# A transformer block with adaLN: the first turn's weights taken in separate steps by score slots, and two output copies moved to GpSimd

## The chip, the cores and the metric

One core of one Trainium2 chip runs the whole kernel. The metric is the device time of one execution in microseconds (us). Engines are named as in the profile: PE is TensorE, DVE VectorE, ACT ScalarE, POOL GpSimd, SP SyncE. SyncE computes nothing here: it issues every DMA, in the order of its queue, and an issue whose condition isn't met holds all behind it. All engines take their instructions in the order of their queues.

## What is computed

```python
mod = (silu(c) @ w_mod).reshape(1, 6, 1, 576)        # sa, ca, ga, sb, cb, gb
h = layernorm(x) * (1 + ca) + sa                     # x: 2048 x 576, float32
q, k, v = h @ wqkv                                   # 32 heads of 18
p = softmax(q @ k.T * 18 ** -0.5)
x = x + ga * ((p @ v) @ wo)
h = layernorm(x) * (1 + cb) + sb
x = x + gb * (silu(h @ w1) @ w2)                     # w1: 576 x 4608, w2: 4608 x 576
```

Matmuls keep float32's accuracy by three products of two-part numbers: a weight `w` is split into a high part in fp32r and the rest, and so is the activation; high x high, high x rest and rest x high are summed.

## The kernel before

The 2048 queries go in four blocks of 512. For each block all 32 heads are taken in eight quads of four heads. A **score slot** is one step of attention: a matmul of scores for the maxima of a later part (`psa`, reduced on VectorE, L728), and one of scores with the maximum already subtracted (`psb`, L776), whose exponential ScalarE takes into `pt` (L778); matmuls with the values (`psv`, L813) follow. A quad of a block has 64 slots, a block 512. What follows attention (projection with `wo`, layernorm, the MLP) for block b is dealt out as filler between the slots of block b+1. I call the slots of block 1, 2 and 3, with the MLP of the block before in them, the first, second and third **turn**; the MLP of block 3 runs alone at the end.

The MLP has 36 first-layer weights (128 hidden units each, tile `w1t`) and 36 second-layer ones (`w2t`). The filler takes **pairs** of first-layer weights (`mlp1`, L1011 and after), with their results through SiLU in tiles `g`, and after two pairs the second layer of a **chunk** of four (`mlp2`). Pairs are counted from 0: pair 0 opens the MLP, pair 2 stands just ahead of the first second-layer group, and pairs 3 and 17 bound the later chunks of the turn. The results of the second layer are added to `x`: one half by VectorE (L918); the other is copied by ScalarE into one of two buffers `gt` (L921) and added by GpSimd (L922). Of a pair's two results, ScalarE and VectorE form SiLU in buffers `etmp`, ScalarE writes the high part of `g` (L1037), and GpSimd subtracts it for the rest (L1038), which frees an `etmp` buffer. ScalarE's queue holds all this between the exponentials.

In the first turn the weights come as float32. `weights` (L633) loads each in two halves into a ring of three buffers `raw`, on GpSimd multiplies a half of a second-layer weight by `gb` (L646), casts it to the high part (L647) and subtracts that for the rest (L648), and at its next call stores the split weight to device memory. From the second turn on one DMA loads the stored weight. The order of TensorE's instructions is that of the program, which a planner (`Plan`, the loop at L1476 and after) makes from estimated costs; the other engines' queues are put in order by a scheduler, which moves a load, split or store up to where it thinks that its inputs and buffers are ready.

At the start of a turn the last quad's output is moved by DMAs from `ov` into the rows of `ou` (L841), `o_T` copies each of five blocks `kt`, four of 128 rows and one of 64, into `th` on ScalarE (L894) and forms the rests `tl` on GpSimd (L897), that of the fifth on VectorE (L899), and the projection `psp` follows.

## Time and profile before

| | us |
|---|---|
| median of three runs | 2437.68 (2436.85 to 2441.84) |
| the profiled execution | 2447.21 |
| its span | 2445.4 |
| TensorE busy in the span | 2352.7 (96%) |
| VectorE / ScalarE / GpSimd busy | 1783.8 / 1483.1 / 631.2 |

The first turn lies at about 578 to 1135 us of the span, the second at 1135 to 1656, the third at 1656 to 2158. TensorE's busy time is counted as the union of its matmuls, whose ends are modelled: a busy TensorE may still run below its rate. Its granted clock is a share of 2.4 GHz; 0.5 is 1.2 GHz.

### The profile page before, as it was taken

Reading aid. Unit: us, or ns where it says so; the run is one execution under the profiler, and the core shown is the slowest. Engines: PE = TensorE matmul, PEld = TensorE weight load, DVE = VectorE, ACT = ScalarE, POOL = GpSimd, SP = SyncE. Lnnn points to the kernel's source line nnn. Section 1 sums busy time; section 2 is a strip of 40 time slices with the busy share of each in tenths; the row PEclk is TensorE's granted clock in tenths of the full one; section 3 lists DMA queues with packets and bytes.
Section 4 is the critical chain, followed back from the end, with each engine's and each line's share of the span. In section 5 each row is a group of like instructions: output and inputs, shape, how many; then the busy total and the mean of one; then the engine's idle time right before and its main releaser. Section 6 shows DMA issues by size and latency. Waiting matters only on the chain.

```text
span 2445.4 us, 52248 instructions
## 1 busy us (share of the span) xinstructions
PE 2352.7 (96%) x19952; PEld 1616.0 (66%) x19952; DVE 1783.8 (73%) x3110; ACT 1483.1 (61%) x2736; POOL 631.2 (26%) x763
## 2 busy tenths in 40 slices
PE   6999999998999999999999999999999999989999
PEld 4874444444566667766677677776676776678998
DVE  7887888887867778877888778878878786134333
ACT  4226777775656666766677767776667677722121
POOL 5201011104666566664211111112211111110000
PEclk9989999999989999999999999999999999999999
DMA  7844445445566666665555554454644554326563
GB/s 249 256 151 151 139 148 152 153 146 190 176 198 197 195 215 214 208 219 176 184 173 185 170 171 162 158 181 127 230 161 162 166 192 152 124 90 243 186 214 119
DMA packets 201474, 433.02 MB, mean 177 GB/s; under 512 B 31362, under 2 KB 67618, under 8 KB 201226
## 3 DMA queue, kind: packets, MB, share of 16 engines
q1 hardware_dynamic: 201226, 429.68, 53.2%
q8 instruction: 160, 2.62, 0.5%
q14 instruction: 88, 0.72, 0.1%
HBM read 338.54 MB, written 86.33 MB: 174 GB/s over the span
## 4 chain that ended last, share of the span: by engine, by line
PE 79%; DMA 6%; DVE 6%; POOL 3%; ACT 3%; issue 2%; SPq 1%; ACTq 0%; POOLq 0%; DVEq 0%
PE ps L483 23%; PE psv L813 16%; PE psa L726 12%; PE ps L477 10%; PE psb L776 8%; PE psqk L569 4%; DMA raw<-in_w 3%; DVE mx L728 2%; PE psp L483 2%; PE psv L483 2%; DMA ka<-kscr 1%; PE psqk L483 1%; ACT pt L778 1%; PE psqk L1259 1%; PE psv L1259 1%
## 5 line engine op out<-in xcount | busy, mean ns | idle before, releaser
L728 DVE TENSOR_REDUCE mx<-psa 128x1 f32<-128x512 f32 x2048 | 1318.8, 684 | 311.7 <-PE psb L776 188.6
L778 ACT ACTIVATE pt<-psb 128x512 f32<-128x512 f32 x2048 | 1131.8, 599 | 487.7 <-PE psb L776 325.4
L776 PE MATMUL psb<-qt,kb 56*128 56x512 f32 x2048 | 756.3, 428 | 28.7 <-ACT pt L778 27.4
L726 PE MATMUL psa<-ka,qt 54*128 54x512 f32 x2016 | 702.7, 420 | 9.4 <-DVE mx L728 7.6
L726 PEld LDWEIGHTS psa<-ka,qt 54*128 54x128 f32 x2016 | 337.9, 187 | 302.6 <-DVE mx L728 213.1
L813 PE MATMUL psv<-pt,vt 128*32 128x512 f32 x4096 | 512.8, 603 | 1.0 <-ACT ov L817 0.9
L483 PE MATMUL ps<-w2t,g 64*128 64x288 f32 x4992 | 417.3, 296 | 5.2 <-ACT gt L921 5.0
L483 PEld LDWEIGHTS ps<-w2t,g 64*128 64x128 f32 x4992 | 389.6, 188 | 37.8 <-DVE mx L728 11.7
L776 PEld LDWEIGHTS psb<-qt,kb 56*128 56x128 f32 x2048 | 354.6, 186 | 80.0 <-ACT pt L778 64.4
L483 PE MATMUL ps<-hh,w1t 64*128 64x512 f32 x2160 | 395.7, 394 | 3.0 <-DVE x L918 1.5
L483 PEld LDWEIGHTS ps<-hh,w1t 64*128 64x128 f32 x2160 | 243.2, 185 | 41.4 <-DVE mx L728 9.2
L1038 POOL TENSOR_TENSOR g<-etmp,g 128x512 fp32r<-128x512 f32 x108 | 138.0, 1297 | 419.4 <-ACT g L1037 320.4
L813 PEld LDWEIGHTS psv<-pt,vt 128*32 128x32 f32 x4096 | 99.5, 109 | 214.9 <-issue 207.0
L483 PE MATMUL ps<-hl,w1t 64*128 64x512 f32 x864 | 197.7, 392 | 0.0
L922 POOL TENSOR_TENSOR x<-x,gt 128x288 f32<-128x288 f32 x116 | 92.7, 801 | 404.5 <-ACT gt L921 404.5
L918 DVE TENSOR_TENSOR x<-ps,x 128x288 f32<-128x288 f32 x184 | 83.9, 456 | 122.7 <-PE ps L477 76.9
L477 PE MATMUL ps<-w2t,g 128*128 128x288 f32 x960 | 133.3, 299 | 7.4 <-ACT g L1037 5.9
L477 PEld LDWEIGHTS ps<-w2t,g 128*128 128x128 f32 x960 | 131.0, 191 | 9.9 <-ACT g L1037 6.3
L483 PEld LDWEIGHTS ps<-hl,w1t 64*128 64x128 f32 x864 | 105.3, 186 | 9.8
L1034 ACT ACTIVATE eq<-ps 128x512 f32<-128x512 f32 x36 | 21.6, 600 | 146.3 <-PE ps L477 146.3
L477 PE MATMUL ps<-hh,w1t 128*128 128x512 f32 x360 | 106.9, 390 | 0.5 <-DVE hh L414 0.5
L1035 DVE SCALAR_TENSOR_TENSOR etmp<-etmp 128x512 f32<-128x512 f32 x108 | 82.3, 795 | 30.3 <-ACT etmp L1034 28.7
(141 smaller groups left out, 2026.7 us busy)
## 6 DMA issues: line engine op xcount, KB each, us to landing
w1t<-w1s SPq DMA_DIRECT2D x108, 640.0 KB
w2t<-w2s SPq DMA_DIRECT2D x108, 576.0 KB
kb<-kscr SPq DMA_DIRECT2D x512, 108.0 KB
ka<-kscr SPq DMA_DIRECT2D x504, 108.0 KB
w1s<-w1t SPq DMA_DIRECT2D x36, 640.0 KB
w2s<-w2t SPq DMA_DIRECT2D x36, 576.0 KB
vt<-vscr SPq DMA_DIRECT2D x32, 608.0 KB
qt<-qscr SPq DMA_DIRECT2D x128, 108.0 KB
```

Source lines behind the costliest of these rows:

```text
L477: mm(self.ps[late], lhsT=lhsT, rhs=rhs, start=(i == 0), stop=(i == self.n - 1))
L483: done = mm(self.ps[g], lhsT=lhsT[rows], rhs=rhs[rows], start=(s == 0), stop=(s == 2 * self.n - 1))
L569: mm(qk_ps[0], lhsT=w[b][:, kt, :], rhs=(hTl if a else hTh)[:, kt, n * 512:(n + 1) * 512], start=(i == 0), stop=(i == 13))
L726: mm(ps, lhsT=t["q"][64 * j:64 * j + 54, hp, stt * P:(stt + 1) * P], rhs=t["a" if ("a", kc, hp) in t else "b", kc, hp][64 * j:64 * j + 54, ...
L728: return lambda: nc.vector.tensor_reduce(t["mx"][:, 2 * j + hp, stt, kc:kc + 1], ps, axis=AX.X, op=ALU.max)
L776: state["pe"] = mm(ps, lhsT=t["b", kt // 4, hp][64 * e:64 * e + 56, kt % 4 * P:(kt % 4 + 1) * P], rhs=t["q"][64 * e:64 * e + 56, hp, :], s ...
L778: nc.scalar.activation(t["P"][kt, hp][:, e, :], ps, AF.Exp, scale=SCALE)
L813: mm(t["ps"][32 * h:32 * h + 32, :], lhsT=t["v"][:, c0:c0 + 32], rhs=t["P"][kt, h // 2][:, h % 2, :], start=(kt == 0), stop=(kt == NKT - 1 ...
L918: nc.vector.tensor_add(c["x1"][j][:, hs], ps, c["x1"][j][:, hs])
L922: nc.gpsimd.tensor_add(c["x1"][j][:, hs], c["x1"][j][:, hs], t)
L1035: nc.vector.scalar_tensor_tensor(t, t, 1.0, u, op0=ALU.add, op1=ALU.mult)
L1038: (nc.vector if last else nc.gpsimd).tensor_tensor(g[:, 1, :], t, f(g[:, 0, :]), op=ALU.subtract)
```

## The change

Weights of the first turn are taken in five steps: load half 0, load half 1, split half 0, split half 1, store. `weights` puts the steps in a list, each with the score slot at which it is to be written: 0, 3, 6, 9 and 12 slots after the first, and the first at least six slots behind that of the weight before. The main loop writes what is due (`serve`). A load, and the first instruction of a split, are made to wait for the last `psb` matmul written (`after_pe`), so the scheduler can't move them ahead of that slot. Ahead of matmuls that read a weight, `settle` writes all steps of the list up to that weight's last at once. The requests themselves stand at other places of the filler, second-layer weights earlier than before. The five `wo` weights keep their old way, but for the store, which comes 24 or more slots later. In the first turn the fourth and fifth output block are copied by GpSimd instead of ScalarE, and the rest of the fifth is formed there too; the planner is told later times for both. From the second turn on, eight pieces of the deferred second layer stand ahead of the fourth output block, and eight behind, in place of 16 behind.

```diff
-REST = (16, 8, 0, 0)
+PRE = 8
+REST = (8, 8, 0, 0)
...
+EACH, LAND = 3, 6
...
+    stream = []
+    served = [0]
+
+    def weights(key, w, src, scr, first, gate=None, spread=True):
+
         if not first:
...
         n = w.shape[2] // 2
-        for cs in (slice(0, n), slice(n, 2 * n)):
-            raw = mp["p"].tile([P, 320], F32, tag="raw", name="raw", bufs=3)[:, :n]
-            nc.sync.dma_start(raw, src[:, cs])
+        raws = {}
+
+        def load(h):
...
+            ins = nc.sync.dma_start(raws[h], src[:, h * n:h * n + n])
+            if spread:
+                after_pe(ins)
...
+        def split(h):
+            cs = slice(h * n, h * n + n)
+            raw, hi = raws[h], w[:, 1, cs]
             if gate is not None:
...
-        stores.append((w, scr))
+                ins = nc.gpsimd.tensor_tensor(raw, raw, gate[:, cs], op=ALU.mult)
+                nc.gpsimd.tensor_copy(hi, raw)
+            else:
+                ins = nc.gpsimd.tensor_copy(hi, raw)
+            if spread:
+                after_pe(ins)
+            nc.gpsimd.tensor_tensor(w[:, 0, cs], raw, f(hi), op=ALU.subtract)
+
+        def store():
+            nc.sync.dma_start(f(scr), f(w))
+
+        todo = [lambda: load(0), lambda: load(1), lambda: split(0), lambda: split(1), store]
+        if not spread:
+            for fn in todo[:-1]:
+                fn()
+            stream.append((state["now"] + 24 + 2 * len(stream), len(stream), key, store))
+            return
+        at = served[0] = max(served[0], state["now"])
+        served[0] += 2 * EACH
+        for k, fn in zip((0, EACH, LAND, LAND + EACH, LAND + EACH + 3), todo):
+            stream.append((at + k, len(stream), key, fn))
+        stream.sort(key=lambda it: it[:2])
+
+    def serve():
+
+        while stream and stream[0][0] <= state["now"]:
+            stream.pop(0)[3]()
+
+    def settle(*keys):
+
+        while any(it[2] in keys for it in stream):
+            stream.pop(0)[3]()
...
-        chain([("V", 700), ("V", 260), ("V", 460), ("V", 700)], plan.t + 700, None, lambda at: o.update({("at", b): at + 5500}))
+        chain([("V", 700), ("V", 260), ("V", 460), ("V", 700)], plan.t + 700, None, lambda at: o.update({("at", b): at + (5500 if b else 6500)}))
...
-            weights(w, wo[:, kt, :], wos[kt], b == 0, ga)
+            weights(("wo", kt), w, wo[:, kt, :], wos[kt], b == 0, ga, False)
...
-            chain([("A", 600)], plan.t, None, lambda at: o.update(th=at + 1500))
             n = P if kt < 4 else 64
-            after_pe(nc.scalar.activation(hi[:n], src[:n], AF.Copy))
-            eng = nc.vector if last and kt % 2 == 0 or kt == 4 else nc.gpsimd
+            if b == 0 and kt > 2:
+                o["th"] = plan.t + 2200 * (kt - 2)
+                after_pe(nc.gpsimd.tensor_copy(hi[:n], src[:n]))
+            else:
+                chain([("A", 600)], plan.t, None, lambda at: o.update(th=at + 1500))
+                after_pe(nc.scalar.activation(hi[:n], src[:n], AF.Copy))
+            eng = nc.vector if last and kt % 2 == 0 or b and kt == 4 else nc.gpsimd
...
+                settle(*[("wo", kt) for kt in range(KT)])
...
         for kt in range(KT):
+            if kt == 3:
+                rest(PRE)
             fl.add(1, lambda kt=kt: o_T(kt), need=(lambda: o["at", b]) if kt > 2 else None)
...
-            weights(c["w1", i], w1[i], w1s[i], b == 0)
+            weights(("w1", i), c["w1", i], w1[i], w1s[i], b == 0)
...
-            weights(c["w2", i], w2[i], w2s[i], b == 0, gb)
+            weights(("w2", i), c["w2", i], w2[i], w2s[i], b == 0, gb)
...
+                settle(("w1", i), ("w1", i + 1))
...
+                settle(*[("w2", i0 + n) for n in range(CH)])
...
-        def add_mlp1(i, w2n=()):
+        def w_at(n, *loads):
+
+            for at, load, i in loads:
+                if at == n and i < NFT:
+                    fl.add(0, lambda load=load, i=i: load(i))
+
+        def add_mlp1(i, *loads):
 
             for part in range(NG):
...
-                if part in (0, 2) and i + 2 < NFT:
-                    fl.add(0, lambda n=i + 2 + part // 2: w_load(n))
...
-        def add_mlp2(i0, add):
+                w_at(part, *loads)
+
+        def add_mlp2(i0, add, *loads):
             for j in range(NST):
                 for part in range(len(G2)):
                     add(MMH * len(G2[part]), lambda j=j, part=part: mlp2(i0, j, part), None, {0: pair_need, len(G2) // 2: half_need}.get(part))
-
-        add_mlp1(0)
+                    w_at(j * len(G2) + part, *loads)
+
+        add_mlp1(0, (0, w_load, 2), (2, w_load, 3))
         for i0 in range(0, NFT, CH):
             if i0 + CH < NFT:
-                add_mlp1(i0 + 2, [(NG // 2, i0 + 1)])
-                add_mlp1(i0 + CH, [(0, i0 + 2), (0, i0 + 3)])
-                add_mlp2(i0, fl.add)
-                fl.add(0, lambda i=i0 + CH: w2_load(i))
+                first = ((2, w_load, 4), (7, w_load, 5)) if i0 == 0 else ()
+                add_mlp1(i0 + 2, (0, w2_load, i0 + 1), (4, w2_load, i0 + 2), (9, w2_load, i0 + 3), *first)
+                add_mlp1(i0 + CH, (2, w_load, i0 + 6), (8, w_load, i0 + 7))
+                add_mlp2(i0, fl.add, (2, w_load, i0 + 8), (9, w_load, i0 + 9), (18, w2_load, i0 + 4))
             else:
...
         run_later()
+        serve()
```

GpSimd's queue at the start of the first turn, before. `tl` and `th` are the two parts of the output, `wo` a split projection weight, `ou` the moved output, x the sum.

```order
L647 CAST wo_6652<-raw 128x288
L897 TENSOR_TENSOR tl<-ou,th 128x512 x3
L648 TENSOR_TENSOR wo_6652<-raw,wo_6652 128x288
L897 TENSOR_TENSOR tl<-ou,th 128x512
L922 TENSOR_TENSOR x_6664<-x_6664,gt 128x288
L387 TENSOR_TENSOR r_7237<-ve,mhalf 128x1
```

And with the change:

```order
L937 TENSOR_TENSOR tl<-ou,th 128x512 x3
L660 TENSOR_TENSOR wo_6649<-raw,wo_6649 128x288
L931 CAST th<-ou 128x512
L931 CAST th<-ou 64x512
L937 TENSOR_TENSOR tl<-ou,th 128x512
L939 TENSOR_TENSOR th<-ou,th 64x512
L963 TENSOR_TENSOR x_6660<-x_6660,gt 128x288
```

Two copies and one difference are added ahead of the last `tl`, behind the last split of `wo`.

GpSimd's queue in the first chunk. In the names before, `w1t_8038` and `w1t_8056` are weights 4 and 5, which pair 2 reads, and `g_7991` and `g_7997` the results of pair 0.

```order
L648 TENSOR_TENSOR w1t_8038<-raw_8040,w1t_8038 128x320
L648 TENSOR_TENSOR w1t_8038<-raw_8044,w1t_8038 128x320
L1038 TENSOR_TENSOR g_7991<-etmp_7988,g_7991 128x512
L648 TENSOR_TENSOR w1t_8056<-raw_8058,w1t_8056 128x320
L1038 TENSOR_TENSOR g_7997<-etmp_7994,g_7997 128x512
L647 CAST w1t_8056<-raw_8062 128x320
L646 TENSOR_TENSOR raw_8132<-raw_8132,gb_100 128x288
L648 TENSOR_TENSOR w1t_8056<-raw_8062,w1t_8056 128x320
```

With the change weights 4 and 5 are `w1t_8050` and `w1t_8118`, `w2t_8073` is second-layer weight 2, and `g_8203` is the second result of pair 1.

```order
L1082 TENSOR_TENSOR g_8203<-etmp_8200,g_8203 128x512
L660 TENSOR_TENSOR w1t_8050<-raw_8132,w1t_8050 128x320
L654 TENSOR_TENSOR raw_8225<-raw_8225,gb_100 128x288
L660 TENSOR_TENSOR w1t_8050<-raw_8164,w1t_8050 128x320
L655 CAST w2t_8073<-raw_8225 128x288
L654 TENSOR_TENSOR raw_8235<-raw_8235,gb_100 128x288
L660 TENSOR_TENSOR w2t_8073<-raw_8225,w2t_8073 128x288
L655 CAST w2t_8073<-raw_8235 128x288
L657 CAST w1t_8118<-raw_8241 128x320
L660 TENSOR_TENSOR w2t_8073<-raw_8235,w2t_8073 128x288
L657 CAST w1t_8118<-raw_8246 128x320
L660 TENSOR_TENSOR w1t_8118<-raw_8241,w1t_8118 128x320
```

Weights 4 and 5 were completed around the results of pair 0; now weight 4 is completed behind those of pair 1, and weight 5 last.

SyncE's queue at the same place, with the change; `w1s` and `w2s` are the stored weights, the raw buffers 8241 and 8246 the halves of weight 5.

```order
L663 DMA w2s_106<-w2t_8039 128x1152
L646 DMA raw_8225<-in_w2 128x288
L646 DMA raw_8235<-in_w2 128x288
L663 DMA w1s_105<-w1t_8050 128x1280
L646 DMA raw_8241<-in_w1 128x320
L646 DMA raw_8246<-in_w1 128x320
L663 DMA w2s_106<-w2t_8073 128x1152
L646 DMA raw_8251<-in_w2 128x288
L646 DMA raw_8255<-in_w2 128x288
L663 DMA w1s_105<-w1t_8118 128x1280
```

Weight 5's loads stand behind the store of weight 4, and every raw load waits until the third one before it is split.

GpSimd's queue in a second-layer group of the second chunk, before: `x` is the add that frees `gt`.

```order
L646 TENSOR_TENSOR raw<-raw,gb 128x288 x2
L648 TENSOR_TENSOR w1t<-raw,w1t 128x320
L922 TENSOR_TENSOR x_6664<-x_6664,gt 128x288
L646 TENSOR_TENSOR raw<-raw,gb 128x288
L922 TENSOR_TENSOR x_6666<-x_6666,gt 128x288
L922 TENSOR_TENSOR x_6668<-x_6668,gt 128x288
L647 CAST w2t<-raw 128x288 x3
L648 TENSOR_TENSOR w2t<-raw,w2t 128x288 x2
L922 TENSOR_TENSOR x_6670<-x_6670,gt 128x288
```

And with the change, in such a group:

```order
L963 TENSOR_TENSOR x_6660<-x_6660,gt 128x288
L660 TENSOR_TENSOR w1t<-raw,w1t 128x320
L657 CAST w1t<-raw 128x320
L660 TENSOR_TENSOR w1t<-raw,w1t 128x320
L657 CAST w1t<-raw 128x320
L660 TENSOR_TENSOR w1t<-raw,w1t 128x320
L963 TENSOR_TENSOR x_6662<-x_6662,gt 128x288
L657 CAST w1t<-raw 128x320
L660 TENSOR_TENSOR w1t<-raw,w1t 128x320
L657 CAST w1t<-raw 128x320
L660 TENSOR_TENSOR w1t<-raw,w1t 128x320
L963 TENSOR_TENSOR x_6664<-x_6664,gt 128x288
```

Multiplies of raw loads stood in a row ahead of two of the adds; now each half's operations stand together, and four or five of them are between two adds.

## Rows read from the trace of the kernel before

**Rows 1.** Score matmuls by window: stretch, us, busy PE, PEld, ACT; clock, DMA, GB/s

```profile
727.30:1122.30 395.00, 141.40 (x377) 67.60 (x376) 210.33 (x377) 0.99 0.63 204
1275.50:1643.10 367.60, 135.08 (x375) 66.41 (x374) 210.18 (x375) 1.00 0.52 171
```

**Rows 2.** Waits, first turn; last row second turn: total, times, longest us

```profile
PE psb L776 <- ACT pt L778: 23.3, 12, 7.2
...
ACT gt L921 <- POOL x L922: 22.3, 6, 6.2
...
POOL raw L646 <- DMA raw<-in_w: 88.9, 48, 8.3
...
PE psb L776 <- ACT pt L778: 1.5, 2, 1.2
```

**Rows 3.** Timeline at 712 us: start, us, instruction, count, [idle before, releaser]

```profile
712.43 0.45 SPq L644 DMA_DIRECT2D raw<-in_w  x1
...
713.37 1.55 POOL L646 TENSOR_TENSOR raw<-raw,gb 128x288 f32<-128x288 f32 x2 [1.92 <-DMA raw<-in_w]
...
714.87 0.80 POOL L922 TENSOR_TENSOR x<-x,gt 128x288 f32<-128x288 f32 x1
...
715.70 0.41 ACT L921 ACTIVATE gt<-ps 128x288 f32<-128x288 f32 x1 [4.63 <-POOL x L922]
...
716.65 1.28 PE L776 MATMUL psb<-qt,kb 56*128 56x512 f32 x2 [2.73 <-ACT pt L778]
...
716.97 0.80 POOL L646 TENSOR_TENSOR raw<-raw,gb 128x288 f32<-128x288 f32 x1 [1.31 <-DMA raw<-in_w]
```

**Rows 4.** Timeline at 686 us

```profile
686.80 2.31 DVE L1035 SCALAR_TENSOR_TENSOR etmp<-etmp 128x512 f32<-128x512 f32 x2 [1.66 <-ACT etmp L1034]
...
688.51 0.91 POOL L647 CAST w1t<-raw 128x320 fp32r<-128x320 f32 x1
...
690.32 0.79 PE L776 MATMUL psb<-qt,kb 56*128 56x512 f32 x1 [2.86 <-ACT pt L778]
```

**Rows 5.** Half-clock windows: stretch, us, busy by engine (PE to POOL), PEclk, DMA

```profile
590.00:600.20 10.20, 4.67 (x23) 2.57 (x25) 2.35 (x3) 3.31 (x6) 2.18 (x3) 0.50 0.62 208
689.00:695.80 6.80, 5.49 (x29) 3.35 (x31) 2.80 (x6) 2.97 (x6) 4.61 (x8) 0.50 0.78 269
```

**Rows 6.** GpSimd's groups, first turn: count, busy us, mean ns, idle before

```profile
L648 POOL TENSOR_TENSOR w1t<-raw,w1t 128x320 fp32r<-128x320 f32 x72 | 63.4, 893 | 0.2
L646 POOL TENSOR_TENSOR raw<-raw,gb 128x288 f32<-128x288 f32 x72 | 59.6, 831 | 89.0 <-DMA raw<-in_w 88.9
...
L647 POOL CAST w1t<-raw 128x320 fp32r<-128x320 f32 x72 | 35.6, 501 | 79.4 <-DMA raw<-in_w 54.7 <-PE ps L483 9.7 <-PE psa L726 6.2
```

**Rows 7.** The window of the first turn; columns as in Rows 5

```profile
578.10:1134.70 556.60, 524.15 (x4848) 366.38 (x4847) 430.15 (x714) 359.57 (x661) 333.73 (x456) 0.97 0.62 199
```

**Rows 8.** Timeline behind a pair: the second turn's first, then pair 1

```profile
1218.16 2.78 PE L813 MATMUL psv<-pt,vt 128*32 128x512 f32 x24
...
1219.68 1.29 DVE L1035 SCALAR_TENSOR_TENSOR etmp<-etmp 128x512 f32<-128x512 f32 x2 [0.61 <-ACT etmp L1034]
...
1221.18 1.29 POOL L1038 TENSOR_TENSOR g<-etmp,g 128x512 fp32r<-128x512 f32 x1 [10.48 <-ACT g L1037]
...
669.41 1.92 PE L813 MATMUL psv<-pt,vt 128*32 128x512 f32 x16
...
671.84 0.63 PE L483 MATMUL ps<-hh,w1t 64*128 64x512 f32 x4
```

**Rows 9.** Timeline at the start of the first turn

```profile
588.28 4.39 SPq L841 DMA_DIRECT2D ou<-ov  x5
...
593.54 0.63 ACT L894 ACTIVATE th<-ou 128x512 fp32r<-128x512 f32 x1 [6.44 <-DMA ou<-ov]
...
595.53 1.27 PE L776 MATMUL psb<-qt,kb 56*128 56x512 f32 x2 [7.16 <-ACT pt L778]
...
598.60 0.61 PE L483 MATMUL psp<-wo,th 64*128 64x288 f32 x2
```

More of the change, by code (lines that the diff above doesn't have):

```diff
@@ L629, in add_qk @@
                         fill.add(200, lambda a=mt_: mod_piece(*a), mode="full")
-    stores = []
-    def weights(w, src, scr, first, gate=None):
-        while stores:
-            w_, scr_ = stores.pop()
-            nc.sync.dma_start(f(scr_), f(w_))
+    stream = []
+    served = [0]
+    def weights(key, w, src, scr, first, gate=None, spread=True):
         if not first:
@@ L641, in weights @@
         n = w.shape[2] // 2
-        for cs in (slice(0, n), slice(n, 2 * n)):
-            raw = mp["p"].tile([P, 320], F32, tag="raw", name="raw", bufs=3)[:, :n]
-            nc.sync.dma_start(raw, src[:, cs])
-            if gate is not None:
-                nc.gpsimd.tensor_tensor(raw, raw, gate[:, cs], op=ALU.mult)
-            nc.gpsimd.tensor_copy(w[:, 1, cs], raw)
-            nc.gpsimd.tensor_tensor(w[:, 0, cs], raw, f(w[:, 1, cs]), op=ALU.subtract)
-        stores.append((w, scr))
+        raws = {}
+        def load(h):
+            raws[h] = mp["p"].tile([P, 320], F32, tag="raw", name="raw", bufs=3)[:, :n]
+            ins = nc.sync.dma_start(raws[h], src[:, h * n:h * n + n])
[4 more added lines that the diff above has]
+            raw, hi = raws[h], w[:, 1, cs]
+            if gate is not None:
+                ins = nc.gpsimd.tensor_tensor(raw, raw, gate[:, cs], op=ALU.mult)
[24 more added lines that the diff above has]
+            stream.pop(0)[3]()
     steps = []
@@ L1072, in post @@
                 fl.add(440, lambda kt=kt: h_T(kt), name=["h_T"], need=hT_need, mode="full")
-        def add_mlp1(i, w2n=()):
+        def w_at(n, *loads):
[3 more added lines that the diff above has]
+        def add_mlp1(i, *loads):
             for part in range(NG):
                 fl.add(MMC * len(GR[part]), lambda part=part: mlp1(i, part), need={0: pair_need, NG // 2: half_need}.get(part))
-                for p_, n in w2n:
-                    if p_ == part:
-                        fl.add(0, lambda n=n: w2_load(n))
-                if part in (0, 2) and i + 2 < NFT:
-                    fl.add(0, lambda n=i + 2 + part // 2: w_load(n))
-        def add_mlp2(i0, add):
+                w_at(part, *loads)
+        def add_mlp2(i0, add, *loads):
             for j in range(NST):
@@ L1087, in add_mlp2 @@
                     add(MMH * len(G2[part]), lambda j=j, part=part: mlp2(i0, j, part), None, {0: pair_need, len(G2) // 2: half_need}.get(part))
-        add_mlp1(0)
+                    w_at(j * len(G2) + part, *loads)
+        add_mlp1(0, (0, w_load, 2), (2, w_load, 3))
         for i0 in range(0, NFT, CH):
             if i0 + CH < NFT:
-                add_mlp1(i0 + 2, [(NG // 2, i0 + 1)])
-                add_mlp1(i0 + CH, [(0, i0 + 2), (0, i0 + 3)])
-                add_mlp2(i0, fl.add)
-                fl.add(0, lambda i=i0 + CH: w2_load(i))
+                first = ((2, w_load, 4), (7, w_load, 5)) if i0 == 0 else ()
+                add_mlp1(i0 + 2, (0, w2_load, i0 + 1), (4, w2_load, i0 + 2), (9, w2_load, i0 + 3), *first)
+                add_mlp1(i0 + CH, (2, w_load, i0 + 6), (8, w_load, i0 + 7))
+                add_mlp2(i0, fl.add, (2, w_load, i0 + 8), (9, w_load, i0 + 9), (18, w2_load, i0 + 4))
             else:
-                add_mlp1(i0 + 2, [(1, i0 + 1), (2, i0 + 2), (3, i0 + 3)])
+                add_mlp1(i0 + 2, (0, w2_load, i0 + 1), (4, w2_load, i0 + 2), (8, w2_load, i0 + 3))
         if last:
```

## The prediction

> **What bounds the kernel now.** I read the windows first, then the waits, then single stalls in the timeline. The kernel's three attention turns with MLP work beside them have the same work from the first pair of the second chunk, pair 3, to the last, pair 17; only the first of them loads float weights, splits them on GpSimd and stores them. The stretch from pair 3 to pair 17 takes 395.0 us with 377 score matmuls in the first turn and 367.6 us with 375 in the second [rows 1]. Two score slots are 2 x 367.6/375 = 2.0 us, so the first turn loses 25.4 us there. In the same turn TensorE waits 23.3 us for ScalarE's exponentials against 1.5 us in the second; ScalarE waits 22.3 us for the buffer that GpSimd's x add frees; and GpSimd waits 88.9 us for raw loads [rows 2]. The answer has no wait of TensorE for a weight. So the weights are not late: they stand in the way. One stall shows all links [rows 3]: GpSimd waits 1.92 us for a raw load, multiplies it and a second one, and only then, at 714.87, runs the x add; ScalarE's gt has by then stood 4.63 us in front of the exponentials; TensorE stands 2.73 us. Another such stall, behind g, is 2.86 us [rows 4]. The clock is at half (1.2 of 2.4 GHz) for 6.8 us from 689.0, and for 10.2 us from 590.0 [rows 5]; work done at half clock loses half of that time, 3.4 and 5.1 us.
>
> **The change part by part.** TensorE's order is the same but for the start of three projections, so the time can only move by waits. Splits, loads and stores are the same instructions with the same bytes.
>
> *Later chunks of the first turn.* A split now stands six slots behind its load, about 6 us; from the end of an issue to the multiply that waited for a raw load is 4.1 us at most here (712.88 to 716.97 [rows 3]). So GpSimd should rarely wait for a load, and an x add or g finds at most one or two halves in front of it: a half of a second-layer weight is 0.83 + 0.50 + 0.89 = 2.2 us [rows 6]. Eight weights at six slots are 48 slots a chunk, and a chunk has 375/7 = 53.6, so the pace just holds. GpSimd is busy 333.7 of 556.6 us [rows 7] and stays so. Of the 25.4 us I take 19 as gained. The upper bound is all of it. The lower one is 8: loads can still be late where SyncE stands behind the row maximum's round trip, and each split now also waits for its score matmul, with x and g queued behind it.
>
> *First chunk.* Here the pace does not hold. Ten weights are asked for before pair 2, 60 slots of dealing, and there are fewer than 50, so the matmuls of pair 2 call in at once what is outstanding (the forced call, `settle`). The new orders show what that makes. GpSimd has weight 4's halves around the two g of pair 1, then second weight 2, then weight 5; SyncE loads weight 5 only behind weight 4's store; and pair 2 reads weight 5 from its first matmuls on. In time from the end of pair 1: g can start 3.0 us after the pair (1218.16 to 1221.18 [rows 8], where GpSimd was free). Two g at 1.29 and a cast at 0.50 make 6.1; difference 0.89, multiply 0.83, difference 0.89 make 8.7; store and load issue at 0.4 each, 9.5; landing 2.1 to 4.1 (I take 2.5, near the shorter ones), 12.0; the cast 0.50, second weight 2's difference 0.89, a cast 0.50 and weight 5's difference 0.89 make 14.8. TensorE comes there 2.4 us after the pair (669.41 to 671.84 [rows 8]), so it loses about 12.4 us, in two pieces; between 9 and 15 by the landing and by what overlaps. Then second weight 3 is forced at the first second-layer group: it stands behind the next two g (3.0 + 2.6), two multiplies 1.7, three casts 1.5, three differences 2.7 and possibly a raw load that SyncE issues late: 11.5 us after pair 2, where TensorE arrives after about 6, so 5.5 us (0 to 8). The clock falls as it did before: behind the longer wait as after the 7.16 us one, 5.1 us, behind the shorter 3.4. In all 26.4 us. Gone are that chunk's two old stalls with their half-clock time, 2.86 + 2.73 + 2 x 3.4 = 12.4. Net +14, from -3 (most of it overlaps) to +20.
>
> *Two output copies.* Before, ScalarE's copy of the fourth block waits 6.44 us for the landing of the moved heads, and TensorE stands 7.16 us [rows 9]; with the half clock that is 12.3 us. Moved to GpSimd, the copies hold back ScalarE no more. What is late next is the projection: it now follows one score slot later, reads the fourth and fifth block in its last third, and these still need the landing at 593.5, two casts (0.50 x 512/320 = 0.8 each), a difference of the length of g, 1.29, and the moved 64-row one, 1.29 at most: 597.7, where before the projection began at 598.60 with all of it still to do. TensorE waits inside the projection instead of before it. Gain about 3 us, from -1 to 8. It is queued behind the same GpSimd queue's last split of wo, which was there before too.
>
> *The rest.* The first pair's weights are loaded later than before, beside hl: +1 (0 to 4). In turns two and three eight pieces of the old MLP now run while the heads move: -2 (0 to -4). SyncE's order from the second turn's later part on is the same, and so is the tail's on TensorE.
>
> Sum: -19 + 14 - 3 + 1 - 2 = -9. The profiled execution is 2447.2 us, 9.5 above the median of the three; the saving carries over as it is: 2437.7 - 9 = 2429.
>
> **The rivals.** (a) *The forced calls cost little.* If the landings are at the short end and the splits overlap with score slots that TensorE still has, the first chunk is even or better (-3), and the rest comes at the upper half: -22 - 3 - 3 + 0 - 2 = -30, 2408. For it: no TensorE wait for a weight stands in the lists now. Against it: the order of the queues leaves no way round, since weight 5 waits for a buffer, a store and two g.
> (b) *Slower.* The forced calls cost the whole 32 us (+20 net), the copies nothing, the pair start 4, and the pace gains only the 8 us: +16, 2454; with 11 us gained and 17 lost, about 2446. The mechanism is one place, the wait for weight 5 at pair 2 and what follows it; it decides as soon as it with its half clock costs over 9 us more than counted, or the later chunks keep over half of their loss.
> (c) *The change does not do what it says:* a split waits for its place behind TensorE as long as it waited for the load, x and g stay as late, and both sides cancel: 2433 to 2442.
> (d) *GpSimd and VectorE get in each other's way.* A GpSimd cast takes 0.91 us beside VectorE's two-input products, which take 2.31 for two [rows 4]; its mean is 0.50 [rows 6], and two such products alone take 1.29 [rows 8]. Dealt out evenly, splits meet all 34 products of the turn. At 0.5 us each VectorE is 17 us later in the turn; if TensorE waits for two thirds of that, 11 us, the gain is used up: 2440. Against it: GpSimd is busy for 60% of this turn now, so most meetings are there already.
> The Trainium skill (SBUF — State Buffer, SBUF: two separate sides) says that a VectorE instruction with two SBUF inputs and a GpSimd one exclude each other for a whole instruction; the 0.91 us cast agrees with it, as far as one row can.
>
> **How the numbers follow.** A measurement of this kernel can tell about 0.2%, 4.9 us, from no change: faster is below 2432.8, slower above 2442.6. The forecast, 2429 with 2422 to 2435 as its own range, has 0.40; (a) 0.24; (b) 0.18; (c) 0.12; (d) 0.06. Faster: 0.9 of the forecast's 0.40 and all of (a), 0.60. Slower: (b), 0.18. Within: 0.04 + 0.12 + 0.06 = 0.22. The range leaves out the far end of (a), all of the gains at their bounds, and that of (b): 2406 to 2448.
>
> **What would show it.** Right: in the later chunks GpSimd's waits for raw loads fall from 88.9 us to under 25, ScalarE's for x from 22.3 to under 6, and the stretch between pairs 3 and 17 to about 376 us. TensorE, for the first time, waits for w1t in pair 2, about 12 us in one or two gaps, with half clock behind it, and for w2t in the group after it. The long gap at 588 is gone and a gap of 3 to 6 us stands inside the projection, released by GpSimd. Wrong: no gap over 5 us at pair 2 (then a), or waits for x and g as before, released by TensorE's score matmuls instead of loads (then c).

## The result, and the profile after

The changed kernel is slower: 2446.07 us median of five executions (2445.18 to 2448.32) against 2437.68 us, a ratio of 1.0033 (95% interval 1.0018 to 1.0049). On another chip it was 1.0031 (1.0021 to 1.0041). The forecast was 2429 us.

The profiled execution took 2445.57 us, which is 1.6 us less than the one of before. So these two profiles don't show the loss as a whole, but they show what each stretch does. Here is the first turn in four stretches, as windows: from score slot 512 to pair 0 (the head), pair 0 to pair 3 (the first chunk), pair 3 to pair 17 (the later chunks), pair 17 to pair 18 (the turn's end). The columns are as in [rows 5]. First before, then after.

```profile
575.40:640.70 65.30, 56.59 (x465) 32.49 (x465) 49.12 (x108) 37.72 (x70) 32.24 (x48) 0.92 0.48 157
640.70:727.30 86.60, 79.01 (x664) 54.06 (x662) 63.90 (x100) 52.35 (x97) 57.66 (x76) 0.92 0.60 196
727.30:1122.30 395.00, 378.80 (x3644) 271.97 (x3642) 308.37 (x495) 261.60 (x481) 240.38 (x328) 0.99 0.63 204
1122.30:1206.90 84.60, 81.28 (x798) 54.39 (x796) 68.46 (x136) 55.10 (x101) 26.75 (x35) 0.98 0.55 181
```

```profile
574.80:639.80 65.00, 58.26 (x464) 33.43 (x465) 48.23 (x107) 36.52 (x68) 27.93 (x38) 0.95 0.42 131
639.80:741.00 101.20, 80.97 (x662) 55.21 (x660) 60.34 (x100) 52.05 (x97) 51.69 (x71) 0.87 0.51 166
741.00:1115.00 374.00, 371.37 (x3644) 266.07 (x3641) 304.63 (x495) 261.63 (x481) 245.09 (x334) 1.00 0.68 218
1115.00:1206.20 91.20, 84.42 (x798) 57.99 (x796) 68.90 (x136) 55.20 (x101) 32.53 (x43) 0.93 0.53 179
```

The later chunks give 21.0 us. The first chunk takes 14.6 and the turn's end 6.6; in both the clock is lower (0.87 and 0.93). The head stays as it was. The following waits of the first turn stand against [rows 2]; the list ends at 1134.7 us, ahead of the last waits for weights:

```profile
PE ps L485 <- POOL w1t L657: 13.4, 3, 8.9
PE psb L812 <- ACT pt L814: 3.1, 7, 1.2
PE psp L485 <- POOL tl L937: 2.6, 1, 2.6
PE ps L485 <- POOL w2t L655: 2.5, 2, 2.0
...
ACT gt L962 <- POOL raw L654: 0.5, 2, 0.3
...
POOL raw L654 <- DMA raw<-in_w: 31.0, 14, 7.0
...
POOL raw L654 <- PE psa L762: 26.3, 9, 7.4
```

TensorE's wait for the exponentials fell from 23.3 us to 3.1, ScalarE's for the x add from 22.3 to nothing that is listed; GpSimd's for raw loads from 88.9 to 31.0, with 26.3 new ones for the score slot. In their place TensorE waits for weights (`w1t` and `w2t`), of which the list of before has none. The longest wait is at pair 2. The timeline there (start, us, instruction, count, [idle before, releaser]):

```profile
675.93 4.88 SPq L646 DMA_DIRECT2D raw<-in_w  x2
...
676.45 0.58 ACT L814 ACTIVATE pt<-psb 128x512 f32<-128x512 f32 x1
676.76 1.27 POOL L1082 TENSOR_TENSOR g<-etmp,g 128x512 fp32r<-128x512 f32 x1
...
676.85 0.49 PE L485 MATMUL ps<-hh,w1t 64*128 64x512 f32 x1 [0.74 <-POOL w1t L657]
...
682.05 0.33 SPq L663 DMA_DIRECT2D w1s<-w1t  x1
682.47 2.13 SPq L646 DMA_DIRECT2D raw<-in_w  x2
...
685.78 0.46 POOL L657 CAST w1t<-raw 128x320 fp32r<-128x320 f32 x1 [1.17 <-DMA raw<-in_w]
686.19 0.80 POOL L660 TENSOR_TENSOR w2t<-raw,w2t 128x288 fp32r<-128x288 f32 x1
...
686.28 0.79 PE L485 MATMUL ps<-hh,w1t 64*128 64x512 f32 x2 [8.95 <-POOL w1t L657]
...
688.25 0.79 PE L485 MATMUL ps<-hh,w1t 64*128 64x512 f32 x1 [1.18 <-POOL w1t L660]
```

SyncE issues weight 5's halves from 682.47 on, right behind the store of weight 4; the cast follows at 685.78, and TensorE has stood 8.95 us. At pair 1, whose first matmul starts at 656.11, it is weight 3:

```profile
654.32 0.36 SPq L646 DMA_DIRECT2D raw<-in_w  x1
...
659.74 0.45 POOL L657 CAST w1t<-raw 128x320 fp32r<-128x320 f32 x1 [5.73 <-DMA raw<-in_w]
...
660.25 0.80 PE L485 MATMUL ps<-hh,w1t 64*128 64x512 f32 x2 [3.74 <-POOL w1t L657]
...
662.29 0.79 PE L485 MATMUL ps<-hh,w1t 64*128 64x512 f32 x1 [1.25 <-POOL w1t L660]
```

Its second half is issued at 654.32, 1.8 us ahead of the pair, and its cast can start only 5.4 us later; from 656 to 662 us the DMA engines are busy 92% of the time. At the turn's end it is the last second-layer weight, which stands behind three differences of the output on GpSimd:

```profile
1133.62 2.50 POOL L937 TENSOR_TENSOR tl<-ou,th 128x512 fp32r<-128x512 f32 x2
...
1136.08 0.79 POOL L660 TENSOR_TENSOR w2t<-raw,w2t 128x288 fp32r<-128x288 f32 x1
1136.83 1.26 POOL L937 TENSOR_TENSOR tl<-ou,th 128x512 fp32r<-128x512 f32 x1
...
1136.92 0.84 PE L485 MATMUL ps<-w2t,g 64*128 64x288 f32 x3 [0.67 <-POOL w2t L660]
...
1138.06 1.54 POOL L654 TENSOR_TENSOR raw<-raw,gb 128x288 f32<-128x288 f32 x2
1139.54 0.79 POOL L655 CAST w2t<-raw 128x288 fp32r<-128x288 f32 x2
...
1140.01 2.48 PE L485 MATMUL ps<-w2t,g 64*128 64x288 f32 x5 [2.25 <-POOL w2t L655]
```

These two waits make 2.9 us. The clock is at half from 1133.4 to 1147.1, and TensorE works 10.4 us of that, which loses 5.2 us, where before loses 1.7 (3.4 us at half clock from 1139.6): together 6.4 of the 6.6 us.

### The profile page after: what moved, and what is told of

It is laid out like the page before. It is cut to its first block, busy times and chain, and to the rows that moved or that the text cites. A ratio compares the mean times of both kernels' runs of the same rounds, so it can differ in the third digit from the quotient of the medians.

```text
span 2443.8 us, 52378 instructions
## 1 busy us (share of the span) xinstructions
PE 2349.4 (96%) x19952; PEld 1614.5 (66%) x19952; DVE 1776.0 (73%) x3109; ACT 1481.9 (61%) x2734; POOL 633.7 (26%) x766
## 4 chain that ended last, share of the span: by engine, by line
PE 85%; DVE 6%; DMA 3%; ACT 2%; POOL 2%; issue 1%; SPq 0%; ACTq 0%; POOLq 0%; DVEq 0%
PE ps L485 26%; PE psv L849 18%; PE psa L762 13%; PE ps L479 10%; PE psb L812 9%; PE psqk L571 4%; DVE mx L764 3%; PE psv L485 2%; PE psp L485 1%; PE psqk L485 1%; PE psv L1307 1%; PE psqk L1307 1%; DMA raw<-in_w 1%; PE psp L479 1%; ACT pt L814 1%
## 5 line engine op out<-in xcount | busy, mean ns | idle before, releaser
L485 PE MATMUL ps<-hh,w1t 64*128 64x512 f32 x2160 | 401.7, 397 | 17.5 <-POOL w1t L657 13.4
L485 PEld LDWEIGHTS ps<-hh,w1t 64*128 64x128 f32 x2160 | 247.8, 187 | 57.9 <-POOL w1t L657 14.6
L576 POOL TENSOR_TENSOR qkhl<-qt,qkhl 128x512 fp32r<-128x512 f32 x24 | 31.0, 1292 | 238.9 <-ACT qt L575 185.1
```

Of the source, the lines that this page charges most:

```text
L485: done = mm(self.ps[g], lhsT=lhsT[rows], rhs=rhs[rows], start=(s == 0), stop=(s == 2 * self.n - 1))
```

## The experiments

Ratios are to the kernel before, timed on the same chip in the same rounds. The stretches are read from the windows of each kernel's profiled execution, in us. Where an expectation gives 80, 87 or 89 us for the stretch from pair 17 to 18, it counts from score slot 1024, 4.4 us later than this table.

| kernel | median | ratio (95%) | head | first chunk | later chunks | turn's end |
|---|---|---|---|---|---|---|
| before | | 1 | 65.3 | 86.6 | 395.0 | 84.6 |
| before_again | 2441.26 | 1.0011 (0.9999 to 1.0023) | 65.9 | 84.6 | 393.9 | 84.4 |
| before_third | 2441.38 (one) | | 63.6 | 84.1 | 392.9 | 85.7 |
| after | 2446.07 | 1.0033 (1.0018 to 1.0049) | 65.0 | 101.2 | 374.0 | 91.2 |
| after_again | 2448.14 | 1.0031 (1.0021 to 1.0041) | 68.4 | 99.9 | 374.7 | 90.6 |
| weights_only | 2445.78 | 1.0026 (1.0014 to 1.0038) | 65.2 | 99.9 | 374.3 | 91.4 |
| copies_only | 2444.83 | 1.0012 (0.9997 to 1.0028) | 71.9 | 82.7 | 389.8 | 83.5 |
| pace2 | 2436.53 | 0.9973 (0.9961 to 0.9986) | 70.8 | 85.2 | 375.6 | 90.7 |
| no_gate | 2424.40 | 0.9932 (0.9914 to 0.9950) | 73.1 | 77.5 | 375.8 | 82.8 |
| first_whole | 2432.84 | 0.9973 (0.9962 to 0.9985) | 73.4 | 78.7 | 373.8 | 93.5 |
| first_last_whole | 2433.13 | 0.9969 (0.9957 to 0.9981) | 71.6 | 75.9 | 375.0 | 90.7 |
| head_spread | 2432.56 | 0.9955 (0.9939 to 0.9971) | 66.4 | 82.8 | 375.4 | 93.3 |
| head_end | 2422.84 | 0.9916 (0.9895 to 0.9937) | 64.6 | 84.2 | 374.8 | 84.1 |
| early_requests | 2417.40 | 0.9898 (0.9878 to 0.9917) | 67.3 | 75.6 | 373.0 | 84.2 |

### The two kernels again

No edit.

> The kernel before, unchanged, profiled and timed once more. The two profiled executions on hand differ by 1.6 us only (after 2445.57, before 2447.21), the medians by 8.4 us the other way, and the profiled execution of before lies 9.5 us over its median. Theory A, that execution was an unlucky one: its half-clock stretches (72 us in all, 27 of them in the first turn) come at other places and are shorter in another execution; expected a profiled execution at 2435 to 2441, with a mean granted clock over 0.987 and some 15 to 20 us less at half clock. Theory B, profiling itself costs this program some 9 us: expected 2445 to 2449 again, with the same stretches at half clock, while the timed runs stay at 2434 to 2442.

> The kernel before, looked at a third time. So far its two profiled executions took 2447.2 and 2444.8 us, while 47 others lie at 2430.8 to 2448.7 with a mean of 2440.2. Theory A, chance: a third lies anywhere in this span, likeliest at 2436 to 2443, and its half-clock stretches and its waits in the later chunks differ from the others by some us (pairs 3 to 17: 388 to 395 us). Theory B, the profiled execution of this kernel is always a long one: 2444 or more, pairs 3 to 17 at 394 to 395 as in both.

> The changed kernel, unchanged, once more beside before. Theory A: it is slower by 3 to 8 us on this chip too, and its profiled execution shows the same stretches within 2 us (pair 0 to 3: 101, pairs 3 to 17: 374, pair 17 to 18: 87), since its waits stand at fixed places, while before's come and go by the landing of the raw loads: its times spread less than before's. Theory J, the two kernels are equal and the first comparison was chance: a ratio of 0.999 to 1.001, as the profiled executions on hand (1.6 us apart) say.

The profiled executions of before took 2447.2, 2444.8 and 2441.4 us. Its 84 timed executions in these comparisons lie at 2430.8 to 2449.7 with a mean of 2441.0 and a mean granted clock of 0.987; the shorter ones have the higher clock (a correlation of -0.71; 0.001 of the clock goes with 1.8 us). The second profiled execution lies outside what either theory expected of it (2435 to 2441, 2445 to 2449), the third is in theory A's span and below theory B's 2444. So the first, with a clock of 0.985, was one from the upper end. All three lie above the mean, but the eleven profiled executions of the other kernels lie from 7.0 us below to 5.1 above their kernels' medians, 0.3 above in the mean: chance is the nearer reading, and that profiling adds some us to before alone is not excluded. After is slower on a second chip too, by as much, and its stretches come back within 4 us (2 had been expected); its ten times lie at 2445.3 to 2452.3. Theory A's smaller spread isn't shown: the standard deviation is 2.4 us, that of before beside it 2.7.

### Which part of the change

weights_only is after without the output copies on GpSimd and without the moved pieces of the old second layer:

```diff
-REST = (8, 8, 0, 0)
+REST = (16, 8, 0, 0)
...
-            if b == 0 and kt > 2:
-                o["th"] = plan.t + 2200 * (kt - 2)
-                after_pe(nc.gpsimd.tensor_copy(hi[:n], src[:n]))
-            else:
...
-            if kt == 3:
-                rest(PRE)
```

copies_only is before with the same lines added.

> The change without its two output copies on GpSimd and without the pieces of the old second layer moved ahead of the fourth block: the weights' steps alone. By the two profiles the copies and the pieces moved the time by under 1 us (pair 0 starts at 639.80 after, 640.68 before). Theory A, the weights make all of it: 2446, within 3 us of after, with TensorE's waits for w1t at pairs 1 and 2 (5 and 10 us) and for w2t at the turn's end as in after. Theory C, the copies cost what the profile hides (GpSimd's queue at the turn's start): 2438 to 2441, 5 us or more under after.

> The kernel before with the other part of the change alone: two output copies and a difference on GpSimd in the first turn, and eight pieces of the old second layer ahead of the fourth block in the later ones. The prediction gave it -3 us in the first turn and -2 in the others; the profiles of after and of weights_only say under 1 us, as the gap of 7.2 us ahead of the projection turns into gaps of 3.7 in it. Theory A: within 3 us of before. Theory I, beside the old order of the splits the copies do bring something, since there GpSimd's queue at the turn's start is as in before: 4 to 6 us less than before.

The weights alone make the loss (1.0026, 2445.78 us): theory A. The copies alone bring nothing (1.0012, theory A there too), and not because they do nothing: the wait of 7.16 us ahead of the projection is gone, but x adds and norms, which now come earlier, stand behind the splits of the first weights. The timeline of copies_only:

```profile
627.04 0.45 POOL L648 CAST w1t<-raw 128x320 fp32r<-128x320 f32 x1 [2.68 <-DMA raw<-in_w]
627.57 0.87 POOL L649 TENSOR_TENSOR w1t<-raw,w1t 128x320 fp32r<-128x320 f32 x1
...
628.39 0.79 POOL L927 TENSOR_TENSOR x<-x,gt 128x288 f32<-128x288 f32 x1
...
629.22 0.46 DVE L933 BATCH_NORM_STATS2 st<-x 128x6 f32<-128x288 f32 x1 [3.05 <-POOL x L927]
...
630.76 0.79 PE L727 MATMUL psa<-ka,qt 54*128 54x512 f32 x1 [2.39 <-DVE mx L729]
```

GpSimd waits 2.68 us for a raw load, VectorE 3.05 us for the x add behind it, its row maxima wait with it, and TensorE stands 2.39 us, and 2.47 once more; the head is 71.9 us. In after, where the splits are kept at their slots, TensorE waits 1.3 us in all for these maxima, and the head is 65.0 to 68.4.

### First chunk and turn's end

first_whole, against after (a negative number means load and split at once; the first three weights are asked for with `False`, which does the same):

```diff
-        add_mlp1(0, (0, w_load, 2), (2, w_load, 3))
+        add_mlp1(0, (0, w_load, -2), (2, w_load, -3))
...
+                    add_mlp1(2, (0, w_load, -4), (2, w_load, -5), (NG // 2, w2_load, -1))
+                    add_mlp1(CH, (0, w2_load, -2), (0, w2_load, -3), (2, w_load, 6), (8, w_load, 7))
```

first_last_whole, against first_whole:

```diff
-                add_mlp1(i0 + 2, (0, w2_load, i0 + 1), (4, w2_load, i0 + 2), (8, w2_load, i0 + 3))
+                add_mlp1(i0 + 2, (1, w2_load, -i0 - 1), (2, w2_load, -i0 - 2), (3, w2_load, -i0 - 3))
```

head_spread, against first_whole:

```diff
-        fl.add(0, lambda: w_load(0, False))
-        fl.add(0, lambda: w_load(1, False))
-        fl.add(0, lambda: w2_load(0, False))
+        fl.add(0, lambda: w_load(0))
+        fl.add(0, lambda: w_load(1))
+        fl.add(0, lambda: w2_load(0))
```

head_end, against head_spread:

```diff
+        each = 2 if key in (("w2", NFT - 3), ("w2", NFT - 2), ("w2", NFT - 1)) else EACH
...
-                add_mlp2(i0, fl.add, (2, w_load, i0 + 8), (9, w_load, i0 + 9), (18, w2_load, i0 + 4))
+                add_mlp2(i0, fl.add, *(((2, w2_load, i0 + 4), (26, w2_load, i0 + 5), (31, w2_load, i0 + 6)) if i0 + 2 * CH >= NFT else ((2, w_load, i0 + 8), (9, w_load, i0 + 9), (18, w2_load, i0 + 4))))
...
-                add_mlp1(i0 + 2, (0, w2_load, i0 + 1), (4, w2_load, i0 + 2), (8, w2_load, i0 + 3))
+                add_mlp1(i0 + 2, (1, w2_load, i0 + 3))
```

> After, but the first six first-layer weights and the first four second-layer weights are loaded and split at once at their old places of the program, as in before, and only stored later; the steps by score slots begin with weight 6. Theory A: the 14.6 us that the stretch from pair 0 to pair 3 is longer than before are gone (101.2 to about 87 us), no wait of TensorE for w1t at pair 2, and the stretch from pair 3 to 17 stays at 374: 2431 to 2433. Theory B, the first chunk isn't what makes the change slower in timed runs: within 4 us of after, 2442 or more.

> The last one, and also the last three second-layer weights of the turn loaded and split at once at their old places. Theory A: the wait of 2.25 us for w2t at 1138 us and most of the 13.7 us at half clock from 1133 are gone, 5 to 6 us less than first_whole: 2425 to 2428, under both kernels. Theory D, the half clock at the turn's end comes from the output's move and not from the weight: the same as first_whole within 2 us.

> As first_whole, but the first three weights (w1t 0 and 1, w2t 0) in steps by score slots, as in after; weights 2 to 5 of the first layer and 1 to 3 of the second are taken whole. In first_whole the splits of those three stood ahead of an x add and of a norm's root on GpSimd, and VectorE's maxima waited for these: two gaps of TensorE, 3.1 and 2.1 us, with half clock behind them, and the turn's start up to pair 0 was 8 us longer. Theory A: that stretch comes back from 73.4 to 65 us, the first chunk stays at 79 us or less: 2424 to 2427. Theory F, it is the later store of wo or the whole splits behind it that cost them: 2432 again.

> As head_spread, and the last four second-layer weights of the turn are asked for 10 to 16 score slots earlier (the last three four slots apart), so that all their splits stand ahead of the last two g on GpSimd. Theory A: the stretch from pair 17 to pair 18 falls from 87 or 89 us to the 80 of before, without a wait of TensorE over 2 us for w2t or g: 6 us less than head_spread, 2418 to 2421. Theory D, the longer stretch has to do with the pieces of the old second layer that are moved, or with the clock alone: 85 us or more, within 2 us of head_spread.

With the first chunk's weights taken whole it falls from 101.2 to 78.7 us, and the kernel is faster than before: theory A. The head is then 73.4 us, by the same stall as in copies_only and a longer wait in the projection (3.24 us), and 66.4 again with the first three weights at their slots (head_spread); but the first chunk gave 4 us of that back: weight 5 is late by 2.3 us there, and the exponentials by 4.5, so that the ratio moved from 0.9973 to 0.9955 only: the head came back as theory A says, the time did not. At the turn's end first_last_whole failed: the wait for w2t is gone, but the whole splits put g late in its place, one wait of 3.75 us. Its time is the one that theory D names, for another reason than theory D's. Asking earlier, and at four slots a weight (head_end), takes the end from 93.3 to 84.1 us with the clock at 1.00, and the median falls by 10: the place and pace of the requests made the 6.6 us, not the output's move.

### Pace, waits, or place of the requests

pace2, against after:

```diff
-EACH, LAND = 3, 6
+EACH, LAND = 2, 6
```

no_gate, against after, in `load` and in `split`:

```diff
-            if spread:
-                after_pe(ins)
```

early_requests, against head_end (second-layer weights 0 to 3 are added to those with two slots between halves):

```diff
-        fl.add(0, lambda: w_load(0))
-        fl.add(0, lambda: w_load(1))
+        for i in range(CH):
+            fl.add(0, lambda i=i: w_load(i))
...
-        add_mlp1(0, (0, w_load, -2), (2, w_load, -3))
+        add_mlp1(0, (8, w_load, 4), (13, w_load, 5))
...
-                    add_mlp1(2, (0, w_load, -4), (2, w_load, -5), (NG // 2, w2_load, -1))
-                    add_mlp1(CH, (0, w2_load, -2), (0, w2_load, -3), (2, w_load, 6), (8, w_load, 7))
+                    add_mlp1(2, (1, w2_load, 1), (3, w2_load, 2), (5, w2_load, 3))
+                    add_mlp1(CH, (2, w_load, 6), (8, w_load, 7))
```

> After with one constant changed: a weight every four score slots in place of six, its two halves two slots apart. Theory A, the pace is what makes weights 4 and 5 late (ten weights at six slots are 60 slots where fewer than 50 are): with 40 slots the forced call at pair 2 has little left, its wait of 10.1 us falls under 4, the turn's last wait for w2t goes too, and the time is 2432 to 2438. Theory E, it is the ring of three raw buffers and SyncE's order, in which a load stands behind the store ahead of it, that makes them late: waits at pairs 1 and 2 stay over 10 us in all, 2442 to 2447.

> After, without the waits that tie each load and each first instruction of a split to the score matmul of its slot; requests and steps stay where they are, and the scheduler may again move them ahead. Theory G, the order that these waits force is what brings the later chunks their 20 us: multiplies of raw loads gather ahead of x and g again, ScalarE waits for x as before (22 us in the turn) and pairs 3 to 17 take 388 us or more. The first chunk loses its waits for w1t at pairs 1 and 2, about 15 us with their half clock, so the time is 2440 to 2450. Theory H, the new places of the requests do it: pairs 3 to 17 stay under 380 us, the first chunk gets its 15 us back, 2425 to 2432.

> As head_end, but no weight is taken whole (save wo): in the first chunk the steps by score slots begin with all four weights of pairs 0 and 1 (w1t 0 to 3), then w2t 0, then weights 4 and 5 of the first layer from the middle of pair 0 on, so that their last splits fall four slots ahead of pair 2, and w2t 1 to 3 in pair 1 at four slots each. Theory A, the first chunk of after was late by the place of its requests alone: no wait of TensorE over 1 us for w1t or w2t from pair 0 to pair 3, that stretch 76 to 79 us (101.2 after, 84.3 head_end), and the time 5 us under head_end: 2416 to 2420. Theory E, the ring of three raw buffers and SyncE's order make them late wherever they are asked for: a wait of 5 us or more for w1t at pair 1 or 2 and 2425 or more.

A faster pace removes the wait at pair 1 and those for w2t in the first chunk, but not the one at pair 2, and at the turn's end it makes the wait for w2t longer, one of 5.95 us:

```profile
673.52 7.72 SPq L646 DMA_DIRECT2D raw<-in_w  x2
...
682.40 0.33 SPq L646 DMA_DIRECT2D raw<-in_w  x1
683.24 0.45 POOL L657 CAST w1t<-raw 128x320 fp32r<-128x320 f32 x1 [0.87 <-DMA raw<-in_w]
683.75 0.80 PE L485 MATMUL ps<-hh,w1t 64*128 64x512 f32 x2 [9.93 <-POOL w1t L657]
...
1131.43 0.61 PE L485 MATMUL ps<-w2t,g 64*128 64x288 f32 x2 [5.95 <-POOL w2t L655]
```

The first line joins two issues. The second, weight 5's first half, stands until 680.9 for a raw buffer, which GpSimd's difference of weight 4 frees then, and its second half follows at 682.40: at that place theory E. The time, 2436.53, is in theory A's span, but neither of the two waits that A named falls. Without the waits for the score slot (no_gate) the first chunk falls to 77.5 us, and, against theory G, the later chunks stay at 375.8, though GpSimd's queue is again blocked by raw loads as in before. The waits of no_gate from 727 to 1122 us:

```profile
POOL raw L652 <- DMA raw<-in_w: 72.0, 40, 6.2
...
ACT gt L958 <- POOL x L959: 2.3, 1, 2.3
PE psb L808 <- ACT pt L810: 2.1, 3, 1.2
```

In the same window of before it is 76.1, 17.7 and 9.1 us. So the new places of the requests and the order of the steps bring the later chunks their gain, not the ties; which of the two does it, no run tells apart. With the requests where after has them, the ties are what makes the first chunk late. They help in the head: without them TensorE waits there 5.0 us for the row maxima, with them 1.3, and it takes 73.1 us against 65.0 to 68.4 in after. But pace2, tied too, has 70.8 at a clock of 0.86, so a part of that difference is the clock's. Asked for early enough, the tied steps do no harm in the first chunk either. The windows of early_requests:

```profile
576.80:644.10 67.30, 59.78 (x465) 33.90 (x465) 48.22 (x106) 36.55 (x68) 27.85 (x38) 0.92 0.40 126
644.10:719.70 75.60, 73.44 (x664) 50.12 (x661) 61.96 (x100) 52.08 (x97) 57.05 (x77) 0.98 0.72 237
719.70:1092.70 373.00, 370.13 (x3644) 267.07 (x3642) 303.07 (x495) 261.53 (x481) 240.82 (x328) 1.00 0.67 217
1092.70:1176.90 84.20, 81.01 (x800) 54.64 (x798) 68.24 (x136) 55.52 (x101) 32.66 (x43) 0.98 0.57 190
```

The list of its waits has none of TensorE for a weight left in the turn, and the kernel is the best of all, 1.0% under before: 2417.4 us. So theory A holds: the place of the requests (with the pace of four second-layer weights) made the first chunk late.

## Why the prediction was wrong

The forecast missed by 17 us. Two terms of the sum failed: it had no term for the turn's end, which cost 6.0 us, and it gave the two output copies 3 us of gain, where their stretch shows 1.8 us of loss. Turns two and three, for which it had 2 us, gave nothing. Most of the rest lies in the execution that the sum was anchored to. Each in turn:

**What bounds the kernel** was right: x and g behind the splits. The wait chain is gone in after, and with it the later chunks' loss.

**Later chunks, -19:** measured -21.0 between the first two profiles, -19.6 between the means of the three of before (393.9) and the two of after (374.4). The size was right, the reason half of it: no_gate shows that the ties to the slots aren't needed for it, and that GpSimd may go on waiting for raw loads (72.0 us) where ScalarE waits for x only 2.3.

**First chunk, +14:** measured +14.6 (+15.5 between the means). The place was right; that the sum came out is in part luck. Pair 2 cost 0.74 + 8.95 + 1.18 = 10.9 us of waiting, not 12.4, and the second layer 4.0 in four pieces, not 5.5, while pair 1 cost 3.74 + 1.25 = 5.0 that the prediction didn't have. At half clock are 27.3 us in three stretches where 17 had been counted, but TensorE works only 15.9 us of them, which loses 8.0 us; 8.5 had been counted.

**Output copies, -3:** measured for the head -0.3 between the first two profiles, +1.8 between the means (65.0 and 68.4, before 63.6 to 65.9). Inside the projection TensorE now waits 0.6 + 2.6 + 0.5 = 3.7 us, as forecast. Mis-sized was the old stall: it was charged with half of 10.2 us at half clock, 12.3 us in all, but the clock fell at 590.0 and TensorE stood till 595.53, so only 4.7 us of work ran at half clock, 2.3 us were lost, and the stall cost 9.5. That is 2.8 of the 3 us. By its waits alone the head should have gained still; it did not, since TensorE is busy there 58.3 us in place of 56.6 for the same matmuls, and why stays open. (The 1 us for the first pair's later start lies in this stretch too.) Without the weights' steps the copies cost the head 7 us: the part of the projection that comes earlier meets GpSimd's splits (copies_only).

**Turns two and three, -2:** nothing. From the third turn's first score slot to its first pair it is 82.2 us before and 82.3 after; for the second turn the pieces lie in the stretch called the turn's end, where copies_only, which has them, stands at 83.5 and before at 84.4 to 85.7.

**The turn's end, no term:** +6.0 between the means. The sum stopped at pair 17. That the last three second-layer weights are asked for in a pair of about twelve slots, at six slots each and with twelve more for the last one's steps, stood in the change; weights_only has the stretch at 91.4, head_end at 84.1, so this was the cause. With it the sum would have been -3 in place of -9. None of the signs that the prediction named looks at this place, so most of them came true (no long gap at 588 us, the waits at pair 2 and behind it, x in time; GpSimd's waits for raw loads at 31.0 us in place of under 25) while the time went the other way.

**The anchor.** The sum was made against an execution of 2447.2 us, which the prediction itself put 9.5 over the median, and the whole of the difference was taken as common to both kernels ("the saving carries over as it is"). It isn't: the profiled executions of after lie 0.5 us below and 2.2 above their medians, those of before 9.5 and 3.5 above and 2.3 below. The measured stretches add up to +1.8 + 15.5 - 19.6 + 6.0 = +3.7 us between the mean profiles, where the sum had -9: 12.7 of the 17 us. Outside the first turn the mean profiles agree within 0.2 us. The timed kernels differ by some 7.5. Where the other 4 us are isn't settled: the three profiled executions of before average 2444.5, 3.5 over the mean of its timed ones, which is likelier chance than profiling. That before's waits come and go from one execution to the next while after's stand at fixed places, as after_again expected, isn't shown.

**The rivals.** The mechanism of (b), the wait for weight 5, was there at about the counted price and did not decide; the slower result came from the turn's end and the anchor, for which no rival stood. That (b) names 2446, the measured time, is luck: neither of its two conditions came true, and its 11 gained and 17 lost make 2444 from the anchor. (a) fell: the forced calls cost what they were said to. Of (c) only its first half is seen: GpSimd's splits now wait 61.2 us for score matmuls (26.3 of it before multiplies), where they waited 11.9, but their waits for loads fell by more, from 143.6 to 59.4 us, and x and g are not late. (d) has the other sign: VectorE's busy time in the later chunks fell from 308.4 to 304.6 us, and the cast of w1t takes 462 ns where it took 501. VectorE's two-input products, 0.65 us each where two stood alone [rows 8], took 1.01 us in the mean there before and 0.84 after. The rule of the Trainium skill (SBUF — State Buffer, SBUF: two separate sides) that the two engines exclude each other may hold for each meeting, but the trace shows less of it than before.

## What to carry to other kernels

Here, steps dealt out evenly cured a queue that was blocked in its middle, but they made the start and the end of the run late, where there wasn't yet, or no longer, room for the deal: cost these two places by themselves, and ask earlier there before changing the pace. Tie a transfer to a place only where moving ahead does harm: here that was at most one place, the head. When half clock is counted behind a wait, count only the work that runs in it. And before a difference of 0.5% is predicted from one profiled execution, ask how that execution stands to the timed ones.

## What the runs showed of the hardware

At the turn's end of after the clock fell to half (1.2 of 2.4 GHz) at 1133.4, 1.9 us behind a wait of 1.23 us, and stayed there for 13.7 us, in which the waits of 0.67 and 2.25 us lie; in head_end, with waits of 1.22 and 2.19 us there and none for w2t, no such stretch is recorded (clock 1.00). Which of the waits brought the clock down, no run tells. A half clock that falls while TensorE still waits costs nothing until the wait ends: at the head of before that holds for 5.5 of 10.2 us, in the first chunk of after for some 11 of 27.3, waits within the stretches counted. And a raw load that was issued with the DMA engines about 90% busy (654.3 to 659.7 us in after) took 5.3 us to land, while one of the same size at pair 2, at a busy share of 0.78, took 3.2 (3.25).
